# Attention in front of two expert layers on one core: one branch instead of two, a smaller mask, and part of the weight unpacking and of the sums of squares in other places

## The chip, the cores and the metric

The kernel runs on one core of one Trainium2 chip. The metric is the device time of one execution, in microseconds (us). Engines: PE (TensorE, matrix products and transposes), DVE (VectorE), ACT (ScalarE), POOL (GpSimd) and SP (SyncE, which here only issues DMAs). PSUM is the memory that PE writes its results to; a result must be copied ("evacuated") from there to SBUF before PE can use it again as an input.

## The reference, cut to what matters

```python
def _attn_ref(q, k, v, n_global, n_local):          # batch 2, 8 heads, 768 rows, 64 wide; 8 and 96
    scores = np.matmul(q, k.transpose(0, 1, 3, 2)) / np.sqrt(D)
    rel = pos[:, None] - pos[None, :]
    is_global = pos[None, :] < int(n_global)
    is_local = (rel >= 0) & (rel < int(n_local))
    keep = is_global | is_local
    dist = np.where(is_global & ~is_local, float(n_local), np.abs(rel))
    scores = scores - slopes[:, None, None] * dist   # one slope per head
    scores = np.where(keep, scores, -1000000000.0)
    a = softmax(scores)                              # written out, with 1e-9 in the divisor
    return np.matmul(a, v)

def _moe_ref(x, w_gate, w_val, w_out, rms_g):       # x: 1536 tokens x 512, inner width 1536
    rms = np.sqrt(np.mean(x * x, axis=-1, keepdims=True) + 1e-06)
    xn = x / rms * rms_g
    g = xn @ w_gate
    return (g * sigmoid(g) * (xn @ w_val)) @ w_out
...
# then _moe2_ref: each token whose x @ w_skip is positive goes through one of 8 experts
```

Weights come as 64-bit floats. `n_global` and `n_local` are inputs, too: the kernel has a path for small windows (these inputs take it) and a general one, and a comparison on the device picks between them.

## The kernel before, in words

**Attention.** With these windows a block of 64 query rows needs two or three blocks of 64 keys beside the first one, so the work is cut into 24 items: 8 pairs of heads times 3 groups `g` of 256 query rows. `attention` (L189) is a generator over t = 0 to 27 that keeps five items in flight. In one round t it issues the score products of item t (`qk`, L225, matrix product at L235), the transposes of item t-2 (`trans`, L276, L281), the products with v of item t-3 (`pv`, L294, L315), on DVE the step that adds mask and bias and takes the maximum (`ttr`, L246), on ACT the exponential (`exp`, L257), on DVE and POOL the normalisation (L262 to L274), and for item t-4 the scaled copies `xh`, `xl` and the squares that the next layer needs (L408 to L410). Six transposed blocks of 128 columns of an item are evacuated in two copies of three blocks, one by DVE (L290) and one by ACT (L292); for the groups 0 one block of the first copy is absent. The order on each engine is the order in which the generator issues.

**The start.** SP issues the loads of numbers, mask (`rel`), q, k and v of head pairs 0 and 1. `consts` (L44) makes an identity, a tile of ones and the flag that says whether the fast path applies; `bias_tiles` (L91) makes the mask's `miss` tile with three operations over 576 columns and then a bias tile per pair of heads, four operations each (L109). At L988 every engine reads the flag and branches around the general attention. Behind the attention, at L1039, every engine branches a second time, around the general form of the sums.

**Weights.** A unit is a 128x512 tile of 64-bit weights. `unpack` (L467) turns it into a high and a low 32-bit part in five steps: an absolute value on ACT (L472), four integer and select steps on DVE (L474, L479, L481, L484), then a cast on ACT (L486) and a difference (L487) on POOL. In the loop of L1023 one step of the generator `unit` is taken per round: unit 0 at t = 9 to 13, unit 1 at t = 14 to 18, unit 2 from t = 24. Unit 3 is taken behind the second branch (`run(unit)`, L1047).

**The second layer's start.** `products(s, 0, 0, 0, 512)` (`s.first`) are the first 32-bit weight products. They fill PE where attention has little left, from t = 24 on. The sums of squares are 14 products with a column of ones (`stats`, L429, L434), all issued at t = 26 and 27 with one weight product behind each; their result goes through `root` (L439), which is a chain of small DVE operations, to `spread` (L454), whose transpose `rp` (L458) on PE stands in the middle of further weight products.

## Time and profile before

| What | Value |
|---|---|
| median of 3 runs | 532.28 us (532.10 to 532.71) |
| the profiled execution | 534.08 us, its span 532.4 us |
| PE busy | 507.1 us, 95% of the span, 3353 instructions |
| DVE busy | 396.4 us, 74% |
| ACT busy | 267.1 us, 50% |
| POOL busy | 151.1 us, 28% |
| DMA | 86.69 MB, 163 GB/s over the span |

The profiled execution is 1.8 us over the median; 1.7 us of it lie outside the span. Rows of a timeline give the start and the duration of an instruction (or of several alike, "x4"), and in brackets how long the engine had been idle and what the profile thinks released it. "PEclk" is the granted clock of PE as a share of 2.4 GHz. An engine's queue is in order: an instruction that waits holds up all those behind it on that engine.

### The profile page before, as it was taken

The numbers are of one execution on the slowest core, as the hardware profiler recorded it, in microseconds if no ns is written. First come the engines' busy times: TensorE is split into PE (matmuls) and PEld (weight loads), VectorE is DVE, ScalarE is ACT, GpSimd is POOL, SyncE is SP. The second block draws the span as 40 slices with busy tenths as digits, with TensorE's granted clock in tenths as the row PEclk, the third lists the DMA queues.
The fourth block names the chain that finished last, engine by engine and source line by source line (L and its number), as shares of the span: only waits on it lengthen the run. The fifth ranks groups of instructions, "written<-read, shape, count | busy, mean of one in ns | idle before, by whom it ended". The sixth has DMA issues, their size and how long they took to land. (4 is left out here: it accounts for less than half of the span.)

```text
span 532.4 us, 9653 instructions
## 1 busy us (share of the span) xinstructions
PE 507.1 (95%) x3353; PEld 412.0 (77%) x3353; DVE 396.4 (74%) x992; ACT 267.1 (50%) x615; POOL 151.1 (28%) x202
## 2 busy tenths in 40 slices
PE   3799999999999999999999999999999999999994
PEld 2576668888888888878888887878898778888883
DVE  6789986478887688688854467767744699999961
ACT  2799994142333323233323524425531779888750
POOL 4477783012222312212112000000000603665001
PEclk9899999999999999999999999999999999999999
DMA  7699821313322423323226113313771899999200
GB/s 239 213 321 292 243 64 41 100 58 102 119 86 85 133 93 119 113 84 115 83 81 218 77 42 120 118 41 128 239 274 39 331 399 396 400 400 393 82 14 17
DMA packets 31454, 86.69 MB, mean 163 GB/s; under 512 B 3907, under 2 KB 4175, under 8 KB 31400
## 3 DMA queue, kind: packets, MB, share of 16 engines
q1 hardware_dynamic: 26856, 74.65, 40.9%
q0 software_dynamic: 2672, 8.22, 4.1%
q10 hardware_dynamic: 1872, 3.15, 1.7%
q8 instruction: 28, 0.46, 0.4%
q14 instruction: 26, 0.21, 0.1%
HBM read 78.31 MB, written 8.66 MB: 163 GB/s over the span
## 5 line engine op out<-in xcount | busy, mean ns | idle before, releaser
L523 PE MATMUL ps<-xh,wh 128*128 128x512 f32 x272 | 106.5, 391 | 0.1
L523 PE MATMUL ps<-xl,wh 128*128 128x512 f32 x272 | 106.3, 391 | 0.0
L523 PE MATMUL ps<-xh,wl 128*128 128x512 f32 x272 | 106.3, 391 | 0.0
L851 DVE TENSOR_TENSOR ewl<-eraw,ewh 128x1024 fp32r<-128x1024 f32 x72 | 83.4, 1217 | 7.5 <-ACT ewh L842 7.3
L842 ACT CAST ewh<-eraw 128x1024 fp32r<-128x1024 f32 x72 | 71.4, 1054 | 6.8 <-DVE ewl L851 6.2
L474 DVE SCALAR_TENSOR_TENSOR wraw<-f64t,wraw 128x512 f32<-128x512 f32 x36 | 44.4, 1232 | 30.0 <-ACT f64t L472 30.0
L601 PE MATMUL px<-woh,hh 128*128 128x512 f32 (+1 forms) x156 | 61.2, 392 | 0.0
L487 POOL TENSOR_TENSOR wl<-f64t,wh 128x512 fp32r<-128x512 f32 x24 | 31.1, 1296 | 101.3 <-ACT wh L486 66.8
L523 PEld LDWEIGHTS ps<-xh,wh 128*128 128x128 f32 x272 | 51.1, 188 | 11.0 <-DVE h L543 0.6
L523 PEld LDWEIGHTS ps<-xl,wh 128*128 128x128 f32 x272 | 51.1, 188 | 10.4
L523 PEld LDWEIGHTS ps<-xh,wl 128*128 128x128 f32 x272 | 51.1, 188 | 10.3
L601 PE MATMUL px<-woh,hl 128*128 128x512 f32 (+1 forms) x156 | 58.4, 374 | 0.0
L601 PE MATMUL px<-wol,hh 128*128 128x512 f32 (+1 forms) x156 | 58.2, 373 | 0.0
L486 ACT CAST wh<-f64t 128x512 fp32r<-128x512 f32 x24 | 14.9, 623 | 71.2 <-DVE f64t L484 71.2
L257 ACT ACTIVATE es<-es,m 128x192 f32<-128x192 f32 (+1 forms) x96 | 41.5, 448 | 6.9 <-DVE m L246 6.7
L274 POOL TENSOR_SCALAR es<-es,z 128x192 f32<-128x192 f32 (+1 forms) x94 | 38.2, 426 | 17.6 <-DVE z L266 6.0
L555 DVE TENSOR_TENSOR hl<-h,hh 128x256 fp32r<-128x256 f32 x72 | 25.4, 423 | 17.8 <-ACT hh L554 17.8
L235 PE MATMUL sc<-kd,qd 64*64 64x192 f32 (+2 forms) x384 | 23.0, 351 | 13.1 <-DVE keep L104 6.8
L601 PEld LDWEIGHTS px<-woh,hh 128*128 128x128 f32 x156 | 29.4, 188 | 5.5 <-issue 0.9
L601 PEld LDWEIGHTS px<-woh,hl 128*128 128x128 f32 x156 | 29.3, 188 | 5.6
L601 PEld LDWEIGHTS px<-wol,hh 128*128 128x128 f32 x156 | 29.4, 189 | 4.1
L541 ACT ACTIVATE sg<-h 128x512 f32<-128x512 f32 (+1 forms) x37 | 22.5, 609 | 18.7 <-DVE h L539 18.7
(215 smaller groups left out, 1020.6 us busy)
## 6 DMA issues: line engine op xcount, KB each, us to landing
eraw<-in_w_dram SPq DMA_DIRECT2D x64, 512.0 KB, 11.1
wraw<-in_wgv_dram SPq DMA_DIRECT2D x24, 512.0 KB, 3.8
wraw<-in_w_out_dram SPq DMA_DIRECT2D x12, 512.0 KB, 3.4
vp<-in_vx_dram SPq DMA_DIRECT2D x8, 704.0 KB, 8.1
eraw<-in_w_dram POOLq DMA_DIRECT2D x8, 512.0 KB, 15.6
kd<-in_kx_dram SPq DMA_DIRECT2D x7, 464.0 KB, 8.9
xm<-x SPq DMA_DIRECT2D x12, 256.0 KB, 2.8
out_dram<-x ACTq DMA_DIRECT2D x12, 256.0 KB, 2.7
```

Of the source, the lines that this page charges most:

```text
L235: nc.tensor.matmul(sc[x][o, r, 0:n], lhsT=qs[pr][d, i:i + 64], rhs=ks[pr][d, k0:k0 + n], start=True, stop=True)
L257: nc.scalar.activation(e[:, r, e0:e0 + n], e[:, r, e0:e0 + n], AF.Exp, bias=m[:, j:j + 1], scale=-1.0, accum_out=z[:, j:j + 1])
L274: eng.tensor_scalar(e[:, r, e0:e0 + n], e[:, r, e0:e0 + n], z[:, j:j + 1], one[0], ALU.mult, *one[1:])
L474: nc.vector.scalar_tensor_tensor(out=a.bitcast(F32), in0=t, scalar=F64_LEAST, in1=a.bitcast(F32), op0=ALU.is_ge, op1=ALU.mult)
L486: nc.scalar.copy(hi, t)
L487: eng.tensor_tensor(lo, t, f(hi), ALU.subtract)
L523: nc.tensor.matmul(p, lhsT=w[:, k, :], rhs=x[c][:, k, a:b], start=n == 0, stop=n == 11)
L541: nc.scalar.activation(sg, u, AF.Silu)
L555: nc.vector.tensor_tensor(hl[:, i, :], src, f(hh[:, i, :]), ALU.subtract)
L601: nc.tensor.matmul(p, lhsT=h[:, k, :], rhs=w[k][:, c:c + N], start=n == 0, stop=n == 35)
L842: eng.copy(wh, raw)
L851: eng.tensor_tensor(wl, raw, f(wh), ALU.subtract)
```

## The change

It has seven parts.

1. `consts` is split. The new `numbers` makes the flag with three operations of POOL; the flag is read at t = 0, the branch ahead of the attention is gone, and the one behind the attention (now L1074) holds the general attention as well, which uses tiles that exist anyway.
2. The mask: `rel` has 648 columns for 1160 (162 KB for 290), `keep` is gone, `miss` takes one operation over all columns and two over the 64 columns of the global keys, and a bias tile takes two operations instead of four.
3. The memsets of `vlo` go from POOL to DVE, ahead of its first work.
4. Products of the ones tile with itself, whose result nobody reads, are put on PE: 10 ahead of the first scores, then 7, 4, 3 and 2 behind the transposes of t = 0 to 3.
5. DVE evacuates four transposed blocks of an item and ACT two.
6. A table `UNPACK` says how many steps of the unpacking each round takes. Unit 0 stays; unit 1 moves from t = 14 to 18 to t = 23, 24 and 25, and its difference from POOL to DVE; unit 2 has two of its steps in t = 26 and 27 and the others behind the branch.
7. Six of the 14 sums of squares move to t = 16, 17 and 18, into a free part of the bank of `po`; the other eight stay at t = 26 and 27, each with two weight products.

```diff
+UNPACK = {9: 1, 10: 1, 11: 1, 12: 1, 13: 1, 23: 1, 24: 3, 25: 1, 26: 1, 27: 1}
...
+    P = nc.gpsimd
+    a = c.tile([128, 2], F32, name="fasta")
+    P.tensor_scalar(a[:, 0:1], s.nl, 1.0, None, ALU.is_ge)
+    P.tensor_scalar(a[:, 1:2], s.nl, float(FAST_LOCAL), a[:, 0:1], ALU.is_le, ALU.mult)
     s.fasti = c.tile([128, 1], I32, name="fasti")
-    nc.vector.tensor_copy(s.fasti, s.fast)
+    P.tensor_scalar(s.fasti, s.ng, float(FAST_GLOBAL), a[:, 1:2], ALU.is_le, ALU.mult)
+
+
+def product(s, out, n):
+
+    for _ in range(n):
+        s.nc.tensor.matmul(out, lhsT=s.ones, rhs=s.ones, start=True, stop=True)
...
-    spans = [(0, 64, 0), (64, 192, 4), (192, 384, 0), (384, 576, 4)]
-    nc.vector.tensor_scalar(keep, rel, s.nl, None, ALU.is_lt)
-    nc.vector.scalar_tensor_tensor(out=keep, in0=key, scalar=s.ng, in1=keep, op0=ALU.is_lt, op1=ALU.max)
-    nc.vector.tensor_scalar(miss, keep, 1.0, -8.0 * NEG, ALU.subtract, ALU.mult)
+    spans = [(0, 256, 0), (256, 576, 4)]
+    nc.vector.tensor_scalar(miss, rel, s.nl, 8.0 * NEG, ALU.is_ge, ALU.mult)
+    key = s.rel[:, N:N + 64].rearrange("p (a b) -> p a b", a=2)
+    for a in range(2):
+        first = miss[:, 256 * a:256 * a + 256].rearrange("p (a b) -> p a b", a=8)[:, 0:6:5, :]
+        nc.vector.scalar_tensor_tensor(out=first, in0=key, scalar=s.ng, in1=first,
+                                       op0=ALU.is_ge, op1=ALU.mult)
...
     def trans(it, r):
-        pt = s.ps_n.tile([128, 3, 128], F32, name="pt", tag="rb", bufs=2)
+        n = 4 - 2 * r
+        pt = s.ps_n.tile([128, n, 128], F32, name="pt", tag="rb", bufs=2)
...
+        if t < 4:
+            product(s, unread, (7, 4, 3, 2)[t])
...
-    flag = nc.values_load(s.fasti[0:1, 0:1], min_val=0, max_val=1,
-                          skip_runtime_bounds_check_because="a comparison's result")
-    with tc.If(flag == 0):
-        general_attention(s)
...
-            yield from split_unit(s, unit, nc.gpsimd)
+            yield from split_unit(s, unit, nc.vector if n == 1 else nc.gpsimd)
...
-        if 9 <= t < 19 or t > 23:
-            next(unit, None)
+        if t in UNPACK:
+            some(unit, UNPACK[t])
+        if 17 <= t < 20:
+            mean(s, spare, 2 * t - 34, 2 * t - 32)
+        if 16 <= t < 19:
+            spare = s.spare
+            run(rms[0].stats(t - 16, spare))
         if t == 26:
-            for x, g in ((0, 0), (0, 1), (0, 2), (1, 0), (1, 1)):
-                for _ in rms[x].stats(g, ss):
-                    some(s.first, 1)
+            for g in range(2):
+                for _ in rms[1].stats(g, ss):
+                    some(s.first, 2)
...
     with tc.If(flag == 0):
+        general_attention(s, s.ps_m, ps_o)
         for x in rms:
             x.general(s.xg)
...
-    root(s, ss)
+    mean(s, ss, 6, 12)
+    some(s.first, 24)
+    root(s)
```

**Where instructions stand now, 1: PE at the start of the second pair of heads.** PE before, from the end of round 2 on: L235 are score products, L281 transposes, L315 the first products with v.

```order
L235 MATMUL sc_437<-kd,qd 64x192
L281 MATMUL pt<-ident,es_369 128x128 x5
L235 MATMUL sc_482<-kd,qd 64x64
L235 MATMUL sc_483<-kd,qd 64x128 x2
L235 MATMUL sc_482<-kd,qd 64x64
...
L281 MATMUL pt<-ident,es_370 128x128 x6
L315 MATMUL po<-pts,vlo_83 64x64 x2
```

The same place now (L250 the scores, L299 the transposes, L334 the products with v, L85 the products that nobody reads):

```order
L250 MATMUL sc_263<-kd,qd 64x192
L299 MATMUL pt<-ident,es_88 128x128 x5
L85 MATMUL unread<-ones 128x128 x3
L250 MATMUL sc_309<-kd,qd 64x64
L250 MATMUL sc_310<-kd,qd 64x128 x2
...
L299 MATMUL pt<-ident,es_89 128x128 x6
L85 MATMUL unread<-ones 128x128 x2
L334 MATMUL po<-pts_279,vlo_82 64x64 x2
```

Three products stand ahead of the scores of t = 3 and two ahead of the first product with v.

**2: DVE from the last rounds of the attention to the root.** Before (L290 evacuation, L410 `xl`, L474 to L484 the unpacking of unit 2 and, behind the branch's rows, unit 3, L443 the root's first operation):

```order
L290 COPY pts<-pt 128x384
L410 SCALAR_TENSOR_TENSOR xl_356<-po,rg,xh_355 128x256
L474 SCALAR_TENSOR_TENSOR wraw<-f64t,wraw 128x512
L410 SCALAR_TENSOR_TENSOR xl_341<-po,rg,xh_340 128x256
L479 TENSOR_SCALAR f64t<-wraw 128x512
L410 SCALAR_TENSOR_TENSOR xl_341<-po,rg,xh_340 128x256
L481 SCALAR_TENSOR_TENSOR f64t<-wraw,f64t 128x512
L1039 COMPARE_AND_BRANCH
...
L484 SCALAR_TENSOR_TENSOR f64t<-wraw,f64t 128x512
L474 SCALAR_TENSOR_TENSOR wraw<-f64t,wraw 128x512
```

Now (L308 evacuation, L434 `xl`, L501 to L511 the four steps, L514 the difference of unit 1):

```order
L308 COPY pts_1635<-pt 128x512
L434 SCALAR_TENSOR_TENSOR xl_176<-po,rg,xh_175 128x256
L511 SCALAR_TENSOR_TENSOR f64t<-wraw,f64t 128x512
L514 TENSOR_TENSOR wl_1578<-f64t,wh_1577 128x512
L434 SCALAR_TENSOR_TENSOR xl_161<-po,rg,xh_160 128x256 x2
L501 SCALAR_TENSOR_TENSOR wraw<-f64t,wraw 128x512
L1074 COMPARE_AND_BRANCH
...
L506 TENSOR_SCALAR f64t<-wraw 128x512
L508 SCALAR_TENSOR_TENSOR f64t<-wraw,f64t 128x512
L511 SCALAR_TENSOR_TENSOR f64t<-wraw,f64t 128x512
L501 SCALAR_TENSOR_TENSOR wraw<-f64t,wraw 128x512
```

Between the last evacuation and unit 2's last step there are now five unpacking operations and one difference, where there were three operations and the last step; the root follows unit 3 as before.

**3: ACT at the same place.** Before (L292 evacuation, L408 `xh`, L409 squares):

```order
L292 COPY pts<-pt 128x384
L408 ACTIVATE xh_340<-po,rg 128x256
L409 ACTIVATE sq<-po 128x256
L408 ACTIVATE xh_340<-po,rg 128x256
L409 ACTIVATE sq<-po 128x256
L1039 COMPARE_AND_BRANCH
```

Now (L310 evacuation, L513 the cast of unit 1, L499 the absolute value of unit 2):

```order
L310 COPY pts_1639<-pt 128x256
L513 CAST wh_1577<-f64t 128x512
L432 ACTIVATE xh_160<-po,rg 128x256
L433 ACTIVATE sq<-po 128x256
L499 ACTIVATE f64t<-wraw 128x512
L432 ACTIVATE xh_160<-po,rg 128x256
L433 ACTIVATE sq<-po 128x256
L1074 COMPARE_AND_BRANCH
```

The last two `xh` now stand behind the cast of unit 1 and the absolute value of unit 2.

## Rows read from the trace of the kernel before

**Rows 1.** The windows view: stretch, us, busy of PE, PEld, DVE, ACT, POOL, then PEclk, DMA share, GB/s.

```profile
17.00:18.00 1.00, 0.05 (x4) 0.08 (x5) 0.96 (x5) 0.55 (x3) 0.00 (x0) 1.00 0.18 52
18.00:21.00 3.00, 3.00 (x28) 2.13 (x30) 1.60 (x10) 1.33 (x7) 1.63 (x4) 0.51 0.04 18
26.00:39.00 13.00, 13.00 (x252) 9.67 (x250) 10.74 (x57) 13.00 (x55) 9.88 (x23) 1.00 1.03 318
41.00:51.00 10.00, 8.95 (x164) 6.24 (x157) 9.78 (x41) 9.69 (x39) 7.82 (x16) 1.00 1.02 284
...
97.00:520.00 423.00, 420.62 (x2031) 346.19 (x2030) 317.57 (x648) 193.33 (x341) 89.39 (x70) 1.00 0.44 159
```

**Rows 2.** The timeline of PE at the start: scores of rounds 0, 3, 4, 5.

```profile
6.82 1.34 PE L235 MATMUL sc<-kd,qd 64*64 64x64 f32 x16 [6.82 <-DVE keep L104]
...
17.95 1.28 PE L235 MATMUL sc<-kd,qd 64*64 64x64 f32 x16 [3.21 <-DVE z L262]
...
21.85 0.88 PE L235 MATMUL sc<-kd,qd 64*64 64x192 f32 x16
...
24.55 0.88 PE L235 MATMUL sc<-kd,qd 64*64 64x192 f32 x16
```

**Rows 3.** The timeline of DVE: round 0's first step, one at 17.75, rounds 5, 10, 15, 21.

```profile
9.75 0.22 DVE L246 CUSTOM_DVE_ANT_0 es<-sc,bias 128x64 f32<-128x64 f32 x1 [0.39 <-DVEq L988]
...
17.75 0.16 DVE L262 TENSOR_SCALAR z<-z 128x4 f32<-128x4 f32 x1
...
25.60 0.36 DVE L246 CUSTOM_DVE_ANT_0 es<-sc,bias 128x192 f32<-128x192 f32 x1
...
39.16 0.36 DVE L246 CUSTOM_DVE_ANT_0 es<-sc,bias 128x192 f32<-128x192 f32 x1
...
55.00 0.23 DVE L246 CUSTOM_DVE_ANT_0 es<-sc,bias 128x64 f32<-128x64 f32 x1
...
72.77 0.23 DVE L246 CUSTOM_DVE_ANT_0 es<-sc,bias 128x64 f32<-128x64 f32 x1
```

**Rows 4.** DMA issues at the start: tile, queue, count, KB, us to landing.

```profile
rel<-in_rel_dram SPq DMA_DIRECT2D x1, 290.0 KB, 3.8
...
qd<-in_qx_dram SPq DMA_DIRECT2D x1, 384.0 KB, 10.6
```

**Rows 5.** The timeline of ACT, round 6: an evacuation of 384 columns, squares of 256.

```profile
30.41 0.48 ACT L292 COPY pts<-pt 128x384 f32<-128x384 f32 x1
...
31.14 0.39 ACT L409 ACTIVATE sq<-po 128x256 f32<-128x256 f32 x1
```

**Rows 6.** DVE's evacuations, L290: ns min/median/max, first and last start, forms.

```profile
L290 DVE COPY pts<-pt x22: 419/552/555, 16.0 to 79.3; 128x384 f32<-128x384 f32 x14, 128x256 f32<-128x256 f32 x8
```

**Rows 7.** The sums of squares, L434, the same columns (two rows for each product).

```profile
L434 PE MATMUL ss<-ones,sq x28: 166/250/271, 86.8 to 92.9; 128*128 128x1 f32 x28
```

**Rows 8.** The timeline of DVE from the last evacuation to the root's last step.

```profile
84.61 0.56 DVE L290 COPY pts<-pt 128x384 f32<-128x384 f32 x1 [2.01 <-PE pt L281]
...
85.47 0.68 DVE L474 SCALAR_TENSOR_TENSOR wraw<-f64t,wraw 128x512 f32<-128x512 f32 x1
...
88.25 0.68 DVE L481 SCALAR_TENSOR_TENSOR f64t<-wraw,f64t 128x512 uint32<-128x512 uint32 x1
89.07 0.69 DVE L484 SCALAR_TENSOR_TENSOR f64t<-wraw,f64t 128x512 uint32<-128x512 uint32 x1
...
97.40 0.17 DVE L451 SCALAR_TENSOR_TENSOR r<-rt,r 128x12 f32<-128x12 f32 x1
```

**Rows 9.** The timeline of ACT: the cast of unit 2, the absolute value of unit 3.

```profile
89.80 0.62 ACT L486 CAST wh<-f64t 128x512 fp32r<-128x512 f32 x1 [2.09 <-DVE f64t L484]
90.33 0.66 ACT L472 ACTIVATE f64t<-wraw 128x512 f32<-128x512 f32 x1
```

**Rows 10.** The timeline of PE: the transpose that needs the root.

```profile
97.72 0.27 PE L458 MATMUL rp<-ident,r 128*12 128x128 f32 x1 [0.28 <-DVE r L451]
```

**Rows 11.** The unpacking's first step over the whole kernel: ns min/median/max.

```profile
L474 DVE SCALAR_TENSOR_TENSOR wraw<-f64t,wraw x36: 682/1350/1681, 41.1 to 266.8; 128x512 f32<-128x512 f32 x36
```

More of the change, by code (lines that the diff above doesn't have):

```diff
@@ L278, in trans @@
         e = st[it][1]
-        pt = s.ps_n.tile([128, 3, 128], F32, name="pt", tag="rb", bufs=2)
-        for k in range(1 if g == r == 0 else 0, 3):
-            nc.tensor.transpose(pt[:, k, :], e[:, r, 128 * k:128 * k + 128], s.ident)
-        pts = ap.tile([128, 3, 128], F32, name="pts", bufs=4)
+        n = 4 - 2 * r
+        pt = s.ps_n.tile([128, n, 128], F32, name="pt", tag="rb", bufs=2)
+        first = 1 if g == r == 0 else 0
+        for k in range(first, n):
+            i, j = divmod(4 * r + k, 3)
+            nc.tensor.transpose(pt[:, k, :], e[:, i, 128 * j:128 * j + 128], s.ident)
+        pts = ap.tile([128, n, 128], F32, name=f"pts{r}", bufs=2)
         outs[it, r] = (pt, pts)
@@ L295, in pv @@
         pr, g = it
-        pts = outs.pop((it, r))[1]
+        pts = [(outs[it, z // 4][1], z % 4) for z in range(3 * r, 3 * r + 3)]
         if r == 0:
@@ L326, in attention @@
                ap.tile([128, 2, 5, 64], F32, name=f"vhi{z}", bufs=1)) for z in range(3)]
+    es += [ap.tile([128, 2, 384], F32, name=f"es{z}", bufs=1) for z in range(3)]
     load(0)
@@ L340, in attention @@
             qk(a, t)
+        if t == 0:
+            unread = s.ps_m.tile([128, 128], F32, name="unread", tag="misc", bufs=1)
         if c:
@@ L982, in attn_moe_kernel @@
     s.ps_g = pool(gctx, "ps_g", space=PSUM)
-    consts(s, ints)
+    consts(s)
+    unread = s.ps_m.tile([128, 128], F32, name="unread", tag="misc", bufs=1)
+    product(s, unread, 10)
+    next(att)
+    numbers(s, ints)
     bias = bias_tiles(s)
     next(bias)
-    flag = nc.values_load(s.fasti[0:1, 0:1], min_val=0, max_val=1,
-                          skip_runtime_bounds_check_because="a comparison's result")
-    with tc.If(flag == 0):
-        general_attention(s)
     xctx = ExitStack()
@@ L1022, in attn_moe_kernel @@
     s.first = products(s, 0, 0, 0, 512)
+    s.mean = s.rpool.tile([128, 12], F32, name="rv", bufs=1)
     for t in att:
```

94 lines of the change are left out of this document (47 added, 47 removed).

## Prediction

> **What bounds the kernel now.** I read the windows of the first 100 us first, then the timelines of PE and DVE there, then ACT's, and last the way into the second layer. PE is busy for 507.1 of 532.4 us, and from 97 us on it is busy for 420.62 of 423 us [rows 1]. That part issues the same products before and after, so the change can win only in the attention and at its two ends: the first 25 us, and the step into the second layer.
>
> *The start.* PE stands still for 3.21 us ahead of the scores of round 3 at 17.95 [rows 2]. The profile names DVE's step `z` as the releaser, but that step ends at 17.91 [rows 3], 0.04 us before; where a DVE result does release PE, at the root, the step ends at 97.57 [rows 8] and PE starts 0.15 us later, at 97.72 [rows 10]. So I take it for the other thing that these scores need, q and k of the second head pair: q needed 10.6 us from its issue to landing [rows 4], k is issued behind it, and the DMA share falls to 0.18 just there [rows 1]. Behind that gap PE's granted clock is 0.51, so the 1.2 GHz level, for 18 to 21 us [rows 1].
>
> *Rounds 5 to 10* take 13.56 us from 25.60 to 39.16 [rows 3], 2.71 each. Here ACT is busy for 13.00 of 13.00 us and DVE for 10.74 [rows 1]: ACT has no gap. (PE shows 13.00 too, but its ends are modelled.)
>
> *Rounds with unpacking.* With unit 0's steps DVE is busy for 9.78 of 10 us [rows 1]: there DVE bounds. The six rounds from 15 to 21, over which unit 1 passes, take 72.77 - 55.00 = 17.77 us [rows 3], where six at 2.71 would be 16.27.
>
> *The end.* PE's transpose of the root waited 0.28 us for DVE's last step, which ends at 97.57 [rows 8, 10]. So in front of it DVE's chain ends last, by little: whatever makes DVE later there is paid in full, and what PE saves there is worth nothing.
>
> **The change part by part.** Minus is a gain.
>
> *A, start: -0.4 us (0 to -0.8).* Without the first branch and with fewer mask operations, DVE's first step moves ahead of 9.75 [rows 3] by some 3 us. But that is covered by the wait at 17.95 if k's DMA sets it. What then counts is that `rel` has 128 KB less. At the 318 GB/s of a stretch with a DMA share of 1.03 [rows 1] these are 0.4 us; 0 if the loads behind it are not limited by bytes, 0.8 if the queue moves half of that here. The three memsets more on DVE (POOL had them) lie in the time before the first scores, which now wait for a load and not for the branch at 6.82 [rows 2].
>
> *B, PE's clock at round 3: -1.1 us (+0.5 to -1.5).* From the scores of round 3 to those of round 4 pass 21.85 - 17.95 = 3.90 us, from those to the scores of round 5 24.55 - 21.85 = 2.70 at the full clock with more products with v [rows 2]. The same work is therefore worth at least 1.2 us less at 2.4 GHz, at most half of 3.90, 1.95; I take the middle, 1.55. Against it stand the two new products ahead of the products with v: a sum of squares is two rows at a mean distance of (92.9 - 86.8)/27 = 0.226 us for a row with a weight product between each pair [rows 7], so I price a product at 0.225, two at 0.45. That leaves -1.1. The 10, 7, 4 and 3 products of the start lie in time in which PE has nothing else. Whether they keep the clock up is not in the trace; if they don't, the two products are paid at half clock, 0.9, and with A this part is +0.5.
>
> *C, the rounds of the attention: -2.1 us (-1.2 to -2.6).* Unit 1 leaves rounds 14 to 18: 16.27 - 17.77 = -1.5. ACT evacuates 256 columns for 384: an ACT operation takes 0.48 us for 384 columns, 0.39 for 256 [rows 5], so -0.09 in the some 15 rounds that ACT bounds, -1.35. DVE's copy goes from 384 to 512 columns: 0.55 less 0.42 is 0.13 for 128 columns [rows 6], which costs where DVE bounds, the four rounds of unit 0: +0.5. The six sums in rounds 16 to 18 are 12 rows of 0.226, so 1.35 us of PE less the products they stood beside; with ACT as the bound PE has some of that free, but its waits are in order, and I take +0.25 (0 to 1.35). The three small operations `mean` on DVE lie where ACT bounds: nothing, and 0.5 if DVE bounds there. The sum is -2.1.
>
> *D, the step into the second layer: +2.0 us (+0.8 to +2.9).* PE's transposes there depend on attention alone, so I keep the clock of the trace. DVE's copy starts at 84.61 [rows 8] and copy and `xl` together take 0.86, to 85.47 [rows 8]; with 0.13 for the larger copy and 0.7 for unit 1's last step (0.69 [rows 8]) it ends at 86.33. Only then can ACT cast unit 1, 0.53 from one start to the next [rows 9]; the two `xh` of the last rounds and the absolute value of unit 2 are behind that cast on ACT: at 86.9 the first `xh` begins, and after it, its square (0.39 [rows 5] each) and the absolute value (0.66 [rows 9]), which overlap a little, some 1.2 us later, at 88.1, the last `xh`. DVE, which has meanwhile made unit 1's difference, takes its `xl` at 88.6 and unit 2's first step at 89.0. Then 0.7, the branch 0.15 (L481 ends at 88.93, L484 starts at 89.07 [rows 8]), 0.5 and 0.7: unit 2's last step starts at 91.05, where it started at 89.07 [rows 8]. Unit 3 and the root follow as before, so the root is 2.0 us later. At least it is DVE's own added work less the waits that this work fills, +0.8; at most the three steps with two inputs take 0.3 us more each. The eight sums that are left instead of 14 save PE 1.35 us; that is covered by the wait for the root, which grows to 0.28 + 1.35 + 2.0 = 3.6 us. Zero, then, and a gain only if D is wrong.
>
> The rule of the Trainium skill that speaks against the longer jump of the one branch is in "Runtime: NRT & Kernel Launch", section Instruction fetch mechanics: a taken branch to a target outside the pages at hand costs a fetch. By it the branch would stay dearer than 0.15; with the 0.39 us that DVE waited at the first branch [rows 3] as an estimate, the sum would come out 0.25 later. The rows show 0.14 for the second branch, and I keep that.
>
> *Sum:* -0.4 - 1.1 - 2.1 + 2.0 = **-1.6 us**. The profiled execution (534.08) would become 532.5; the runs' median, 1.8 below the profiled one, goes by the same difference from 532.28 to **530.7 us**. What this measurement can tell from no change is about 0.2%, 1.06 us, so from 531.2 to 533.3 is "same".
>
> **The rivals.**
>
> *R1, the change doesn't do what its unread products are for:* PE's clock falls to half again at round 3. For it: a product of one tile gives PE little to do, and the gap there is one of data. Against it: the products fill part of it. Price: A and B together +0.5 for -1.5, so 532.7 us. Chance 0.17.
>
> *R2, the clock falls at the end.* PE waits 3.6 us ahead of the root's transpose. Before, a gap of 3.21 us was followed by a stretch at half clock of some 3.4 us (within 17.95 to 21.85 [rows 1, 2]), 1.7 us lost. For it: the gap is longer. Against it: PE is dense ahead of it, and was not at the start. 530.7 + 1.7 = 532.4 us. Chance 0.12.
>
> *R3, slower: DVE's steps at the end run at their usual length, not their shortest.* The tail above is priced by 0.68 [rows 8], the shortest of L474 (0.682); its median is 1.35 [rows 11]. If the five steps with two inputs between unit 1's last and unit 2's last step run at the median, the root is 5 x 0.65 = 3.25 us later: 533.9 us. The point from which it decides is whether another engine works on SBUF beside them. For it: most of these steps in the kernel are slow. Against it: POOL has only short additions of squares there, now that the difference of unit 1 is DVE's. Chance 0.10.
> By "GPSIMD Engine Reference", section Key points, of the Trainium skill, POOL and DVE share their way to SBUF where a DVE step has two inputs from there; by it the slow steps are those that POOL overlaps, which would keep R3 small here.
>
> *R4, the root isn't later:* ACT takes the cast in a gap and D is zero: 528.7 us. For it: DVE has 2.01 us free ahead of 84.61 [rows 8], in which unit 1's last step could fit if it stood there. Against it: the order puts it behind that copy. Chance 0.10.
>
> *R5, the load isn't what holds round 3:* the named releaser is the true one, and the start's whole 3 us come through: -2.6 more, 528.1 us. Against it: 0.04 us is too short for a release. Chance 0.06.
>
> **How the numbers follow.** The forecast has 0.45 and a range of its own from 529.5 to 531.9, from the bounds of A to D taken together as independent. Two thirds of that lie under 531.2 (0.30), the rest is "same" (0.15). R4 and R5 are faster (0.16), and a few of R1 and R2 come out faster where C is at its better end (0.04): 0.50. R1 and R2 are mostly "same" (0.20), a part of them slower (0.05), R3 is slower (0.08) or just under (0.02): same 0.37, slower 0.13. The range from 528.4 to 533.6 leaves out the far half of R3 and R5 and the far ends of the others.
>
> **What would show it.** A: DVE's first step at some 6.7 us, but round 3's scores not before 17. B: a granted clock near 1 in the window of round 3, and under 3.5 us between the scores of rounds 3 and 4. C: six rounds from 15 to 21 in some 16.3 us, ACT no longer without a gap between 26 and 39 us. D: unit 2's last step some 2 us later against the last evacuation than before (4.46 us from copy to step, then 6.4), and a PE gap of about 3.6 us ahead of `rp`, with the clock still full behind it. It is wrong if the clock is half at round 3 or behind `rp`, if round 3 starts some 3 us earlier than 17.95, or if PE's gap ahead of `rp` is under 2 or over 5 us.

## The result and the profile after

The changed kernel is slower: median 535.93 us (533.15 to 542.20, 15 runs) against 532.71 us (531.88 to 535.27, 15 runs) of the kernel before on the same chip, a ratio of 1.0056 with a 95% interval of 1.0039 to 1.0074, so some 3.0 us. The forecast was 530.7 with 528.4 to 533.6. Runs more than 1.5% over the fastest of a kernel are left out of the ratios; two of the 15 are such. The 15 runs spread over 9 us, where those of before lie within 3.4: much of what follows is about that.

The first trace of the changed kernel (534.18 us, span 532.4, as long as that of before) shows what was gained and lost in a good run. The windows, with the columns of [rows 1] (PE, PEld, DVE, ACT, POOL, then the clock):

```profile
17.00:18.00 1.00, 1.00 (x20) 0.70 (x19) 0.37 (x3) 1.00 (x5) 0.27 (x2) 1.00 1.01 334
18.00:21.00 3.00, 3.00 (x59) 2.46 (x57) 2.80 (x13) 2.84 (x13) 1.54 (x5) 1.00 1.03 383
26.00:39.00 13.00, 12.37 (x250) 9.51 (x252) 11.88 (x58) 12.46 (x52) 10.07 (x23) 1.00 1.04 304
41.00:51.00 10.00, 7.13 (x145) 5.67 (x146) 8.69 (x37) 8.69 (x34) 7.68 (x16) 1.00 0.90 261
96.00:98.00 2.00, 2.00 (x11) 2.00 (x11) 0.28 (x1) 0.00 (x0) 0.00 (x0) 0.50 0.02 3
97.00:520.00 423.00, 420.91 (x2024) 346.70 (x2023) 317.92 (x644) 193.12 (x341) 89.48 (x70) 1.00 0.45 159
```

At the start the clock is full where it was 0.51. But from 26 us on no engine is busy throughout any more (ACT 12.46 of 13.00, then DVE 8.69 of 10, where they had 13.00 and 9.78), so something else holds the rounds: PE stops three times there with no wait that the profile shows ("issue" below). And the clock is 0.50 at 96 to 98 us, a stretch that the kernel before does not have there. The timeline of PE (the scores of rounds 0, 3, 4 and 5, the three stops, and the root's transpose `rp`), then DVE's first step of rounds 3, 5, 10, 15, 20 and 21:

```profile
6.32 1.03 PE L250 MATMUL sc<-kd,qd 64*64 64x64 f32 x16
14.05 0.77 PE L250 MATMUL sc<-kd,qd 64*64 64x64 f32 x16 [0.87 <-DMA kd<-in_kx_dram]
16.98 0.88 PE L250 MATMUL sc<-kd,qd 64*64 64x192 f32 x16
19.68 0.88 PE L250 MATMUL sc<-kd,qd 64*64 64x192 f32 x16
...
33.87 0.55 PE L250 MATMUL sc<-kd,qd 64*64 64x192 f32 x6 [0.63 <-issue]
...
42.13 0.27 PE L334 MATMUL po<-pts,vp 128*64 128x64 f32 x2 [1.13 <-issue]
...
49.96 0.77 PE L250 MATMUL sc<-kd,qd 64*64 64x64 f32 x16 [1.74 <-issue]
...
95.80 0.38 PE L485 MATMUL rp<-ident,r 128*12 128x128 f32 x1 [2.75 <-DVE r L478]
```

```profile
15.42 0.23 DVE L261 CUSTOM_DVE_ANT_0 es<-sc,bias 128x64 f32<-128x64 f32 x1
20.74 0.36 DVE L261 CUSTOM_DVE_ANT_0 es<-sc,bias 128x192 f32<-128x192 f32 x1
34.58 0.36 DVE L261 CUSTOM_DVE_ANT_0 es<-sc,bias 128x192 f32<-128x192 f32 x1 [0.53 <-POOL es L289]
50.90 0.22 DVE L261 CUSTOM_DVE_ANT_0 es<-sc,bias 128x64 f32<-128x64 f32 x1 [0.43 <-PE sc L250]
65.81 0.36 DVE L261 CUSTOM_DVE_ANT_0 es<-sc,bias 128x192 f32<-128x192 f32 x1
68.49 0.22 DVE L261 CUSTOM_DVE_ANT_0 es<-sc,bias 128x64 f32<-128x64 f32 x1
```

Against [rows 2, 3] round 5's first step on DVE is 4.86 us earlier (20.74 for 25.60), round 15's 4.10 (50.90 for 55.00), round 21's 4.28. The root's transpose `rp` is only 1.92 earlier (95.80 for 97.72 [rows 10]): the end has taken 2 us. The rest of the span behind `rp` took 434.6 us before and takes 436.6 now, with PE at half clock for the first 3.3 us of it: there the gain is gone.

DVE's and ACT's timelines of the end answer to [rows 8, 9]:

```profile
80.67 0.68 DVE L308 COPY pts<-pt 128x512 f32<-128x512 f32 x1
81.66 0.68 DVE L511 SCALAR_TENSOR_TENSOR f64t<-wraw,f64t 128x512 uint32<-128x512 uint32 x1
83.02 0.69 DVE L514 TENSOR_TENSOR wl<-f64t,wh 128x512 fp32r<-128x512 f32 x1 [0.69 <-ACT wh L513]
85.27 0.68 DVE L501 SCALAR_TENSOR_TENSOR wraw<-f64t,wraw 128x512 f32<-128x512 f32 x1
87.29 0.69 DVE L511 SCALAR_TENSOR_TENSOR f64t<-wraw,f64t 128x512 uint32<-128x512 uint32 x1
95.58 0.17 DVE L478 SCALAR_TENSOR_TENSOR r<-rt,r 128x12 f32<-128x12 f32 x1
```

```profile
82.37 0.62 ACT L513 CAST wh<-f64t 128x512 fp32r<-128x512 f32 x1 [1.38 <-DVE f64t L511]
83.53 0.67 ACT L499 ACTIVATE f64t<-wraw 128x512 f32<-128x512 f32 x1
84.08 0.48 ACT L432 ACTIVATE xh<-po,rg 128x256 fp32r<-128x256 f32 x1
```

From the last evacuation to unit 2's last step it is 87.29 - 80.67 = 6.62 us, where it was 4.46: the chain over ACT's cast and absolute value that the prediction spelled out.

### The profile page after: what moved, and what is told of

It is laid out like the page before. It is cut to its first block, busy times and chain, and to the rows that moved or that the text cites. A ratio compares the mean times of both kernels' runs of the same rounds, so it can differ in the third digit from the quotient of the medians.

```text
span 532.4 us, 9738 instructions
## 1 busy us (share of the span) xinstructions
PE 511.8 (96%) x3405; PEld 420.1 (79%) x3405; DVE 401.3 (75%) x985; ACT 264.8 (50%) x615; POOL 147.2 (28%) x201
## 5 line engine op out<-in xcount | busy, mean ns | idle before, releaser
L501 DVE SCALAR_TENSOR_TENSOR wraw<-f64t,wraw 128x512 f32<-128x512 f32 x36 | 43.7, 1213 | 28.0 <-ACT f64t L499 28.0
L514 POOL TENSOR_TENSOR wl<-f64t,wh 128x512 fp32r<-128x512 f32 x23 | 29.8, 1294 | 101.0 <-ACT wh L513 66.2
L513 ACT CAST wh<-f64t 128x512 fp32r<-128x512 f32 x24 | 14.9, 621 | 74.7 <-DVE f64t L511 74.7
L289 POOL TENSOR_SCALAR es<-es,z 128x192 f32<-128x192 f32 (+1 forms) x94 | 36.9, 412 | 22.8 <-DVE z L281 10.9
L1280 POOL DMA_INDIRECT early<-xm,si_f x1 | 1.3, 1293 | 106.3 <-DMA eraw<-in_w_dram 106.3
```

The costliest lines, as they stand in the source:

```text
L289: eng.tensor_scalar(e[:, r, e0:e0 + n], e[:, r, e0:e0 + n], z[:, j:j + 1], one[0], ALU.mult, *one[1:])
L501: nc.vector.scalar_tensor_tensor(out=a.bitcast(F32), in0=t, scalar=F64_LEAST, in1=a.bitcast(F32), op0=ALU.is_ge, op1=ALU.mult)
L513: nc.scalar.copy(hi, t)
L514: eng.tensor_tensor(lo, t, f(hi), ALU.subtract)
L1280: nc.gpsimd.indirect_dma_start(out=s.early, out_offset=None, in_=s.xm[0:1152, :], in_offset=bass.IndirectOffsetOnAxis(ap=si, axis=0), boun ...
```

## Experiments

Ratios are to runs of the kernel before on the same chip, with their 95% intervals. Each group of experiments ran on a chip of its own, so kernels of different groups are compared by their ratios. The part of the span behind `rp` is given as the time that passes from `rp`'s start to the end. A "fall" is a stretch in which the granted clock is 0.5, the 1.2 GHz level.

**First group: which part of the end, and what the unread products are worth.** e1 is the changed kernel itself.

> The changed kernel once more, unaltered, to see a second trace and the granted clock of more runs. Theory A (the time lost is PE's clock): time and mean granted clock of the runs go together, some 0.5 us per 0.001, as in the first runs (531.5 us of span at 0.997, 537.8 at 0.984), and the trace shows one or more stretches of 3.4 us at 1.2 GHz, each behind a gap of PE of 2 us or more; the median is 534 to 537 us. Theory B (something else, such as later landings, makes the runs slow, and the clock only follows): runs of equal clock differ by more than 2 us.

Measured: 537.54 us (533.61 to 540.18, 12 runs), ratio 1.0077 (1.0055 to 1.0099). The trace has one fall, behind `rp` again. Neither theory holds alone: the runs with the lowest clocks (0.986, 0.987) are the slowest, but at 0.994 spans go from 531.8 to 536.1.

```diff
-    some(second, 6)
-    spread(s)
-    some(second, 18)
+    some(second, 24)
+    spread(s)
```

> The root's transpose stands behind 18 more weight products of 256 columns, 2.1 us of PE work. Theory A: the gap of PE ahead of it falls from 2.75 us to under 0.8, the clock stays full there, and the median falls by 1.7 us or more against the changed kernel, to 531 to 534 us, with less spread. Theory B: the gap is filled and the time stays within 0.5 us, because the second layer waits for the scaling rows that come out of the root anyway.

Measured: 533.73 us, 1.0022 (1.0000 to 1.0044); against e1 on the same chip that is 3.8 us less. The gap ahead of `rp` is 0.51 us, the clock is full there, and behind `rp` pass 433.8 us (part of that is 18 products that now stand ahead of it). Theory A, at this place.

```profile
98.79 0.28 PE L485 MATMUL rp<-ident,r 128*12 128x128 f32 x1 [0.51 <-DVE r L478]
```

The trace has a fall at the start instead, behind a wait of 2.33 us for q and k.

```diff
-UNPACK = {9: 1, 10: 1, 11: 1, 12: 1, 13: 1, 23: 1, 24: 3, 25: 1, 26: 1, 27: 1}
+UNPACK = {**{t: 1 for t in range(9, 19)}, **{t: 1 for t in range(24, 28)}}
...
-            yield from split_unit(s, unit, nc.vector if n == 1 else nc.gpsimd)
+            yield from split_unit(s, unit, nc.gpsimd)
```

> Unit 1 of the weights is unpacked in rounds 14 to 18 again and unit 2 from round 24, as before the change, and all differences are POOL's; the rest is the changed kernel. Theory A with loads as the bound of the middle rounds: rounds 15 to 18 wait for q and k of the next head pair anyway, so the attention ends at most 0.8 us later than in the changed kernel; the root comes some 2 us earlier against the last evacuation, the gap ahead of its transpose is under 1.5 us and the clock stays full: 531 to 533.5 us. Rival (the forecast's own term): unit 1 costs 1.5 us in these rounds, and the time is within 0.5 us of the changed kernel's runs without a fall of the clock.

Measured: 532.94 us, 1.0012 (0.9991 to 1.0034), 4.6 us under e1. The last evacuation is 0.58 us later than in e1 (81.97 for 81.39), `rp` 1.58 earlier (94.95 for 96.53) with a gap of 0.73 and no fall behind it. Ahead of round 15 the two traces differ by PE's stops and by the landing of the loads, too; counted from DVE's first step of round 15, the last evacuation comes after 30.19 us for 29.50. So the unpacking's new place is worth 0.7 us, which is the net of a larger gain and of its cost in the last rounds, and costs 2.2 from there to `rp`, and the fall on top. The trace is of the fastest of the twelve runs; but of all twelve, seven have a granted clock of 0.995 or more, of the 27 runs of the changed kernel (the 15 above and e1) two.

```diff
-    for _ in range(n):
+    for _ in range(0):
         s.nc.tensor.matmul(out, lhsT=s.ones, rhs=s.ones, start=True, stop=True)
```

> The unread products are left out; the rest is the changed kernel. If they hold the clock at the start: a half-clock stretch shows in rounds 0 to 4, the scores of round 5 start 1 to 2.5 us later than 19.68 and the time rises by up to that, unless the loads take it back later (rounds 15 and 18 wait for them). Rival: the whole gain of the start is the earlier loads; the scores of rounds 3 to 5 start within 0.5 us of the changed kernel's, and the time stays.

Measured: 535.63 us, 1.0046 (1.0029 to 1.0063), 1.9 us under e1 instead of over it. The trace has the half clock at the start, round 5 starts 0.74 us later than 20.74 on DVE (21.48), and the attention is nevertheless a little earlier at its end (last evacuation at 80.25 for 80.67). PE makes no stop without a visible wait, not at the second branch either, and so waits longer ahead of `rp`:

```profile
95.40 0.28 PE L485 MATMUL rp<-ident,r 128*12 128x128 f32 x1 [3.47 <-DVE r L478]
```

No fall follows here, but this is again the fastest of the twelve runs, at a clock of 0.994; the other eleven have 0.982 to 0.992, and there is no trace of one of them. That the kernel without these products is if anything faster fits neither expectation.

**Second group: closing the gap, and the other parts.** e5 joins the edits of e2 and e3.

> Both edits that shorten the gap ahead of the root's transpose together. Theory A (the loss is in that gap: PE time not used, and a fall of the clock behind it): the gap is closed, what the start gained is kept, and the median is 530.5 to 532.5 us, below the kernel before by 0.5 to 2 us. Rival (the rounds of the attention gave back what the start gained, and the end holds only what e3 already took back): 532.5 to 533.5 us, the same as the kernel before.

Measured: 533.96 us, 1.0009 (0.9984 to 1.0035). The twelve runs fall into two sorts: five of 530.46 to 531.74 with clocks of 0.997 and 0.998, seven of 533.74 to 536.38 with 0.991 to 0.995. Its trace is of the second sort. PE waits 3.08 us for q and k at round 3, the clock is half for 6.8 us behind it, and round 5 starts at 25.91, where the same start without a fall gives 20.6 to 21.8. The end is cured, the start not.

```diff
-        if 17 <= t < 20:
-            mean(s, spare, 2 * t - 34, 2 * t - 32)
-        if 16 <= t < 19:
-            spare = s.spare
-            run(rms[0].stats(t - 16, spare))
...
-            for g in range(2):
-                for _ in rms[1].stats(g, ss):
-                    some(s.first, 2)
+            for x, g in ((0, 0), (0, 1), (0, 2), (1, 0), (1, 1)):
+                for _ in rms[x].stats(g, ss):
+                    some(s.first, 1)
```

> All 14 sums of squares stand at rounds 26 and 27 again with one weight product behind each; the rest is the changed kernel. Theory A: 1.35 us of PE work come back into the gap ahead of the root's transpose, which falls from 2.6 to about 1.3 us; the clock falls there in fewer runs, and the median is 1 to 3 us under that of the changed kernel, with the root no later. Rival (PE's gap is only idle time): the root's chain sets the time, and the median stays within 0.7 us of the changed kernel's 535.9 to 537.5 us.

Measured: 533.54 us, 1.0013 (0.9995 to 1.0032). The gap ahead of `rp` is 1.45 us, no fall shows, and behind `rp` pass 434.8 us. The trace is of the fastest run, but nine of the twelve have a clock of 0.996 or more. Theory A. There is a second effect, which I had not put down: the rounds 15 to 19 (to the start of round 20) are 1 us shorter. The first steps on DVE of rounds 15 and 20, of e6 (neither sums nor unit 1 there), of the second trace of the kernel before (unit 1 there; e8 below) and of e3 (both):

```profile
50.30 0.22 DVE L261 CUSTOM_DVE_ANT_0 es<-sc,bias 128x64 f32<-128x64 f32 x1
64.08 0.36 DVE L261 CUSTOM_DVE_ANT_0 es<-sc,bias 128x192 f32<-128x192 f32 x1
```

```profile
53.53 0.23 DVE L246 CUSTOM_DVE_ANT_0 es<-sc,bias 128x64 f32<-128x64 f32 x1
68.29 0.36 DVE L246 CUSTOM_DVE_ANT_0 es<-sc,bias 128x192 f32<-128x192 f32 x1
```

```profile
51.78 0.23 DVE L261 CUSTOM_DVE_ANT_0 es<-sc,bias 128x64 f32<-128x64 f32 x1
67.12 0.36 DVE L261 CUSTOM_DVE_ANT_0 es<-sc,bias 128x192 f32<-128x192 f32 x1
```

These are 13.78, 14.76 and 15.34 us; the changed kernel (sums only) has 14.91, and 14.64 in e1. The other traces without a fall there agree: 13.78 and 13.80 with neither (e12, e18), 14.76 to 14.79 with unit 1 (the first of before, e11, e17), 15.33 with both (e5), and 14.58 to 14.84 with the sums (e2, e4, e7, e9, e10, e13, e14). So unit 1 cost 0.98 us in these rounds, and in the six rounds of the forecast, 15 to 21, 1.22 (17.75 in e8, 16.53 in e6), not 1.5; the six sums cost 0.8 to 1.1, not 0.25: one took the place of the other.

```diff
-        n = 4 - 2 * r
+        n = 3
...
-        pts = [(outs[it, z // 4][1], z % 4) for z in range(3 * r, 3 * r + 3)]
+        pts = [(outs[it, z // 3][1], z % 3) for z in range(3 * r, 3 * r + 3)]
```

> DVE evacuates three blocks and ACT three again, as before the change; the rest is the changed kernel. The forecast's term C: rounds bound by ACT become 0.09 us longer each, some 1.35 us in all, and the four rounds with unit 0 shorter by 0.13 each; the median is 0.5 to 1 us over the changed kernel's. Rival (the loads set the middle rounds): no change in the rounds 10 to 20, the attention ends within 0.4 us of the changed kernel's, and DVE's last copy, which stands in the chain to the root, is 0.13 us shorter: within 0.5 us.

Measured: 535.62 us (9 runs), 1.0052 (1.0028 to 1.0076): the changed kernel's ratio. Rounds 10 to 14 take 15.57 us for 15.84 in e1, so the larger DVE copy costs 0.27 where DVE bounds (0.13 between e18 and e11, whose PE does not stop), half or less of the 0.5 forecast. Rounds 5 to 9 show the smaller ACT copy: 13.27 us with four and two where nothing else stops them (e18), 13.55 with three and three (e11). That is 0.06 a round, not 0.09. In sum the evacuations are worth 0.6 us at most (15 rounds at 0.06 less 0.27), where the forecast had 0.85, and the ratio shows nothing of it.

> The kernel before, unaltered, for a second trace. If the first trace of it (534.08 us, 1.8 over its median) was an unlucky one: the scores of round 3 start 1 us or more ahead of 17.95, because q and k of the second head pair land earlier, and the span is 530 to 531.5 us. If it was a usual one: the scores of round 3 start within 0.5 us of 17.95.

Measured: 532.32 us, span 530.6: the first trace of the kernel before was an unlucky one, as the expectation has it. The second head pair's q lands 6.8 us after its issue, for 10.6 in [rows 4], and PE starts the scores of round 3 without a wait, 3.46 us ahead of 17.95. The timeline of PE, those scores and `rp`:

```profile
14.49 1.34 PE L235 MATMUL sc<-kd,qd 64*64 64x64 f32 x16
...
96.20 0.27 PE L458 MATMUL rp<-ident,r 128*12 128x128 f32 x1 [0.26 <-DVE r L451]
```

But DVE, which has the bias tiles to make, comes to round 3 at 17.93 only, 1.47 us ahead of the first trace; round 5's first step starts at 24.20, the last evacuation at 83.11. The profile has no record of the clock ahead of 21.12 us here; that PE runs at half clock until then is read from its scores, 1.34 us above for 0.77 at 14.05 in the changed kernel.

Against this trace the first one of the changed kernel gains 3.46 us by round 5, 2.44 by the last evacuation and 0.40 by `rp`. Then comes the fall, and behind `rp` pass 436.6 us for 434.4.

**Third group: the start, the loads, and the change cut down.**

```diff
-            product(s, unread, (7, 4, 3, 2)[t])
+            product(s, unread, (7, 4, 10, 2)[t])
```

> Ten unread products instead of three behind the transposes of round 2, some 1.75 us more of PE work ahead of round 3; the rest is the changed kernel. If the clock falls at the start in the runs in which PE waits over 2 us for q and k of the second head pair (2.33, 2.38 and 3.08 us in the traces with a fall, 0.74 to 1.78 in those without): the gap there stays under 1.5 us, no half-clock stretch shows before 90 us, the fall ahead of the root's transpose stays, and the median is 0.5 to 2 us under the changed kernel's, 534.5 to 536 us. Rival (the products only delay the scores): round 3 is up to 1 us later, the median the same or higher.

Measured: 535.37 us (11 runs), 1.0047 (1.0022 to 1.0071). In the trace the wait at round 3 is 0.70 us and there is no fall anywhere, though PE waits 2.75 us ahead of `rp`; round 3 is later by 1.5 us. The median is within the uncertainty of the changed kernel's: inconclusive on time. The fall behind `rp` was expected to stay, and is not in this trace.

```diff
-            load_unit(s, units[1])
+        if t == 18:
+            load_unit(s, units[1])
+        if t == 19:
+            load_unit(s, units[2])
...
-            if n < 2:
-                load_unit(s, units[n + 2])
+            if n == 1:
+                load_unit(s, units[3])
```

> Units 1 and 2 of the weights (512 KB each) are loaded at t = 18 and 19, behind the last loads of q, k and v, instead of at t = 4 and 13; the rest is the changed kernel. If the loads bound rounds 5 to 18: 1 MB less at about 320 GB/s is up to 3.2 us, rounds 5 to 18 take 1.5 to 3 us less than 39.4 us, and the median falls by as much. Rival (engines bound these rounds, loads are only busy): they stay within 0.7 us of 39.4, and the median within 0.7 us.

Measured: 535.05 us, 1.0039 (1.0021 to 1.0057). Rounds 5 to 17 take 39.44 us, 39.37 in the changed kernel. The weights' loads do not bound these rounds.

> Only the start of the change is left: one branch, the flag on POOL, the mask, the memsets on DVE. Three and three evacuations, no unread products, unpacking and sums in their old places. By the account so far the end costs nothing more than before, and the start is up to 3 us earlier in round 5, of which the loads take back some 1 us by round 20: 530.5 to 532 us, under the kernel before by 0.5 to 2 us. Rival (the early loads cost in the rounds what the start wins): 532.4 to 533.5 us.

e11 undoes e3's, e4's, e6's and e7's parts at once. Measured: **531.82 us** (530.62 to 533.70), 0.9981 (0.9966 to 0.9997): faster than the kernel before by 1.0 us. Round 5 starts at 21.71, though the clock is half between 15 and 19 us; the last evacuation is at 80.70, and:

```profile
93.95 0.27 PE L485 MATMUL rp<-ident,r 128*12 128x128 f32 x1 [0.40 <-DVE r L478]
```

That is 2.25 us earlier than in e8. Behind it pass 435.8 us for 434.4; waits of PE of 0.26 and 0.5 us for `h` are a part of that.

> The changed kernel with all sums at the end again, the root's transpose 18 products later, ten unread products at round 2, and units 1 and 2 loaded late. If the clock's falls and the loads are the causes: no half-clock stretch between 10 us and the end of PE's work, rounds 5 to 18 shorter, 528 to 531 us in most runs, under both kernels. Rival: what is closed at one place opens at another, and the median is 532 us or more.

e12 joins the edits of e2, e6, e9 and e10. Measured: 532.34 us (530.57 to 534.76), 0.9981 (0.9964 to 0.9998), under both kernels. By its median the rival holds (532 us or more): the trace has no fall, but PE stops three times, for 1.90, 1.07 and 0.77 us, with no wait that the profile shows. This kernel has 33 unread products and is as fast as e11, which has none.

**Fourth group: both gaps closed, and three more traces of the changed kernel.**

> The changed kernel with ten unread products at round 2 and the root's transpose 18 products later; sums, unpacking and evacuations stay as changed. If the falls at these two places make the difference to the kernel before: median 531 to 533 us, within 1 us of the kernel before, granted clock of the runs mostly 0.995 or more. If something else makes the runs slow: 534 us or more, with clocks of 0.994 or less in half of the runs.

e13 joins e2 and e9. Measured: 533.68 us, 1.0021 (1.0001 to 1.0040), between the two expectations, and the ratio of e2 again. Its trace has a fall at some 37 us, behind a stop of 1.58 us without a visible wait.

> The changed kernel, unaltered, one trace. If the falls are at the two places: each stretch at half clock starts within 12 to 23 us or within 1.5 us of the root's transpose, and the part behind the transpose takes 434.4 to 434.9 us without a fall there, 436.4 to 436.8 with one. If there is a third place, a stretch lies elsewhere.

> The same kernel, a further trace, the same expectations as for the first of these looks.

> The same kernel, a further trace, the same expectations as for the first of these looks.

Measured: 533.34, 541.63 and 538.97 us. e14 has one fall, behind `rp`. e15 has one at the start and a long one at 63 to 73 us, none behind `rp`. e16, whose time lies within those of e1's runs, has three, at the start, at 63 us and behind `rp`. Its PE timeline and windows:

```profile
14.57 0.51 PE L250 MATMUL sc<-kd,qd 64*64 64x64 f32 x10 [2.35 <-DVE z L281]
...
36.59 0.55 PE L250 MATMUL sc<-kd,qd 64*64 64x192 f32 x6 [1.35 <-issue]
...
60.96 0.33 PE L299 MATMUL pt<-ident,es 128*128 128x128 f32 x1 [1.60 <-issue]
62.30 0.61 PE L458 MATMUL po<-ones,sq 128*128 128x1 f32 x4
62.84 1.34 PE L250 MATMUL sc<-kd,qd 64*64 64x64 f32 x16
...
101.02 0.38 PE L485 MATMUL rp<-ident,r 128*12 128x128 f32 x1 [2.54 <-DVE r L478]
```

```profile
15.00:18.00 3.00, 2.94 (x22) 2.22 (x14) 1.90 (x11) 1.96 (x9) 1.37 (x4) 0.51 1.03 227
63.00:66.00 3.00, 3.00 (x30) 2.13 (x32) 1.65 (x10) 2.08 (x9) 0.46 (x2) 0.50 0.80 274
100.00:104.00 4.00, 2.98 (x15) 2.98 (x16) 1.10 (x6) 0.00 (x0) 0.00 (x0) 0.57 0.13 52
```

So there is a third place: the last transpose (x1) of five stands 1.60 us behind the others with "issue" as the reason, in e15 1.90 us, and the clock falls 1.9 and 1.1 us after it starts, next to the sums that were moved there. From DVE's first step of round 17 to that of round 18 pass 5.40 us, 2.94 in e14.

**Fifth group: the unread products by themselves.**

> The kernel of e11 (one branch, mask, memsets; the rest as before the change) with the unread products put back (10, then 7, 4, 3, 2). If they hold the clock at the start and bring the stops of PE: no fall before 20 us, but a stop of 0.6 us or more without a visible wait in rounds 9 to 17, a wider spread of the runs than e11's 530.6 to 533.7, and a median of 532.3 us or more. If they only help: median 531.3 us or less and no such stop.

e17 is e11 with e4's edit taken back. Measured: 535.34 us (532.41 to 537.55), 1.0040 (1.0021 to 1.0059). e11's ratio was 0.9981, so in this pair the unread products cost 0.6%, some 3.1 us. That is the price in this arrangement, not of the products as such: taken out of the changed kernel they gave back 0.3%, 1.9 us (e4 against e1, with intervals that overlap), and e12 with them is as fast as e11 and e18 without (it loads the weights late as well). Two rows of PE's timeline of e17, and the first's counterpart in e11:

```profile
16.59 0.67 PE L250 MATMUL sc<-kd,qd 64*64 64x64 f32 x14 [2.55 <-DMA kd<-in_kx_dram]
...
94.80 0.36 PE L550 MATMUL half<-xh,wh 128*128 128x256 f32 x1 [2.05 <-PEq L1069]
```

```profile
14.08 0.77 PE L250 MATMUL sc<-kd,qd 64*64 64x64 f32 x16 [2.10 <-DMA kd<-in_kx_dram]
```

The clock falls at both of e17's. The first is the wait at round 3, which the products do not bridge; but e11 has a fall there as well (15.12 to 18.53 us), and that e17 is 2.51 us later at this place is the load's landing, which goes by the run (these scores start at 13.8 to 16.6 us in the traces in which they wait for it with unread products, at 13.9 to 15.8 in the three with one branch and without). The second is at the branch behind the attention (L1069 there), and e11 has neither the stop nor the fall. Of the 20 traces, all 15 with unread products have such a stop of PE at that branch, of 0.54 to 2.05 us; the five without them (both of before, e4, e11, e18) have none of 0.3 us. Of stops inside rounds 5 to 23 without a visible wait, of 0.4 us or more, 14 of the 15 have one to four (e7 has none), of the five only the first trace of before has one (0.59 us).

The traces say more of these stops than "issue". They also hold the packets of a queue that the profile calls "instruction" (q8, 28 or 29 of 16,384 bytes). I count the products and weight loads of PE in order, as far as the profile shows them. All 25 stops of 0.4 us or more in the 14 traces then stand at the positions 962, 1218, 1474, 1730 or 2242 (to one), which are multiples of 256 apart, and each ends 1.27 to 1.57 us after such a packet has landed; in e16 the packet ahead of the stop at 60.96 landed at 59.43. The 15 stops at the branch end 1.58 to 1.61 us after one. Position 962 is passed 1.27 to 1.57 us after the packet in every trace with unread products, and 1.97, 2.15 and 3.21 us after it in e4, e11 and e18: there the packet comes early enough.

> The changed kernel without unread products, with all sums at the end and the root's transpose 18 products later; unpacking and evacuations (four and two) as changed. If the falls and the sums' place make the loss: no stop of 0.4 us or more without a visible wait, at most the fall at the start, which the loads cover in part, median 530.5 to 532.3 us, under the kernel before. If the new places of the unpacking or the evacuations cost by themselves: 532.8 us or more.

e18 joins the edits of e2, e4 and e6. Measured: 532.70 us, 0.9989 (0.9970 to 1.0007), between the two expectations. No stop of 0.4 us without a visible wait; PE is at half clock until 21 us as in e8 (the scores of round 3 take 1.34 us, and the record of the clock begins at 21.43); the range of the runs is 530.22 to 534.67. It is not told apart from the kernel before, nor from e11: the unpacking's and the evacuations' new places bring nothing by themselves that these runs can tell.

## Why the prediction was wrong, point by point

- **The sum.** Against e8 the first trace of the changed kernel, whose time is under the median, gains 3.46 us by round 5 (A and B: 1.5 forecast), loses 1.02 from there to the last evacuation (C: a gain of 2.1 forecast), loses 2.04 to `rp` (D: 2.0 forecast), and loses 2.19 behind it (nothing forecast). So D was right, A and B were too small by 2.0, and two steps made a loss of the gain: C, wrong by 3.1, and the clock behind `rp`, which the sum takes as full and only the rival R2 prices. The traces e15 and e16 have falls at round 3 and behind round 17's start on top.
- **What bounds the kernel.** That the scores of round 3 can wait for q and k of the second head pair is right: in the changed kernel the profile names that load. But the gap of 3.21 us from which the forecast starts was of an unlucky run. In the second trace of before PE starts these scores at 14.49 without a wait, and DVE, busy with the bias tiles that the change shortens, comes to them at 17.93 only. So A's step that DVE's 3 us are "covered by the wait at 17.95" failed: the changed kernel's scores of round 3 start at 14.05, which the prediction names as a sign that it is wrong.
- **A and B, forecast -1.5.** Measured -2.5 at round 3 and -3.5 at round 5 against e8, in a run without a fall: right in direction, too small. B's step that the products "lie in time in which PE has nothing else" holds for the time ahead of round 3 and not for what follows: they cost 3.1 us where nothing but they was added (e17 against e11), 1.9 in the changed kernel, nothing that shows in e12. They raise the clock early (the profile's record of full clock begins at 5 to 8 us, without them at 12 to 21), but it falls at round 3 whenever PE then waits longer: with unread products, waits of up to 1.78 us had no fall (nine traces), waits of 2.33 to 3.08 had one (six traces); without them 1.94 and 2.10 had one (e4, e11). R1's mechanism, with a chance of 0.17, was there in six of fifteen traces. And with them PE stops where it did not.
- **C, forecast -2.1.** Measured from round 5 to the last evacuation: 58.91 us in e8, 59.93 in the first trace of the changed kernel, 59.55 in e1, 58.89 in e14, and 63.16 and 66.41 in e16 and e15, with their falls. So 0 to +1.0 without a fall there. e4, which has all of C and no stop of PE, takes 58.77, so the terms come to -0.1 and the stops to the rest, where there is one. The terms: unit 1 -1.2 for -1.5 in the forecast's six rounds, but its steps cost some 0.3 in the last rounds (from round 21 to the last evacuation 12.18 us in the changed kernel and 11.87 in e3), where the forecast put nothing; the sums +0.8 to +1.1 for +0.25; the evacuations -0.6 at most for -0.85. The failing step is that PE's work among rounds bound by ACT is nearly free; the sums were priced near their lower bound and belonged near the upper. The weights' loads, which I suspected in between, did not bound these rounds (e10).
- **D, forecast +2.0.** Measured from the last evacuation to `rp`: 13.09 us in e8, 15.13 in the changed kernel, +2.04. The chain was right link by link (6.62 us to unit 2's last step for 6.4), and so was that PE's saved 1.35 us is worth nothing there. PE's gap ahead of `rp`, 3.6 in the forecast, is 3.47 in e4; in the five traces of the changed kernel the stop at the branch takes 0.82 to 1.06 us of it, and both together are 3.57 to 3.61. As `rp` comes 15.15 us after the last evacuation in e4 and 15.12 to 15.14 in the changed kernel, that stop costs nothing there; in e17, with no wait behind it, it does.
- **R2, the fall behind `rp`, chance 0.12, 1.7 us.** In the traces in which PE waits 2.54 to 2.87 us there, six of eight have the fall, and behind `rp` pass 436.2 to 436.8 us with it, 434.6 and 434.9 without. Its price is some 1.8, the difference of the means. It was forecast as a rival; it was the usual case. e2, e3 and e6 each shorten the gap by another way, and each lowers the ratio by 0.3 to 0.7%, idle time and fall together.
- **Its rivals apart.** I gave R1 and R2 one after the other and each mostly as "same". Together with a third place, they make a run of 537 to 542 us, beyond the range. R3 did not happen: the steps with two inputs took 0.68 to 0.69 us. R4 did not either. R5's reason is false, as the profile names the load `kd`; but its outcome, that the start's whole 3 us come through, is what round 5 shows.
- **The rule on branches.** I kept DVE's 0.14 us and set aside the rule of the Trainium skill, "Runtime: NRT & Kernel Launch", section Instruction fetch mechanics, that a taken branch to a target not at hand has to wait for a fetch of instructions. On DVE that held. On PE the stops of 0.54 to 2.05 us at the branch are what the rule describes. The same section says that an engine fetches its instructions in blocks by a DMA queue of its own; the stops at positions 256 apart, each at nearly the same distance behind a packet of the instruction queue, agree with that, and I read them as waits of PE for its instructions. Why the packets come late with the unread products, and whether the loads that keep the DMA share at 1.0 there delay them, stays open: no run here changes the fetch by itself.

The change as a whole: the branch and the mask alone are worth -1.0 us (e11). Of the rest, no part is shown to gain by itself, the end lost 2.0, and the unread products with the gap at the end brought several places at which the clock may fall. Why e17, which differs from the changed kernel by three parts that go back, is no faster than it, although e3 and e6 alone are, is not shown; its stop at the branch of 2.05 us is the longest of all.

## What to carry to other kernels

Filler products that keep a clock up are not free because PE is idle: price them by a run of their own, in the arrangement that they are to stand in, since they move every instruction behind them (here the price was 3.1 us, 1.9, or nothing that shows), and look whether the wait that they bridge can be longer than they are. A gap in one trace may be of that run alone: take a second trace before building a forecast on it. When work is taken off an engine at the end of a chain, ask what that engine will then wait for: at the full clock the wait costs its length, and a fall behind it cost 1.8 us more here. If runs of the new kernel spread more than those of the old, take several traces before explaining one.

## What was not expected of the hardware

In the six traces with unread products in which PE waited 2.3 to 3.1 us at the start, 1.2 GHz followed for 3.41 us, in e5 for 6.83; stops of 1.58 to 1.90 us without a visible wait had a fall behind them in e13, e15 and e16. But a wait of 3.47 us ahead of `rp` in e4, 2.75 in e9 and 2.60 in e15 had none, nor had stops of 1.74 in the first trace of the changed kernel and 1.90 in e12, so the length of the wait alone does not decide it.

A stop of PE for which the profile names no wait can be one for instructions: here all such stops of 0.4 us or more in the rounds, of up to 1.90 us, ended 1.27 to 1.57 us after a packet of 16,384 bytes on the instruction queue.
